# Attention by two pairs of heads at a time, and a float64 conversion with one instruction fewer on ScalarE

## The chip, the cores and the metric

The kernel runs on one core of one Trainium2 chip. The metric is the device time of one execution in microseconds (us). TensorE (PE in the rows) does the matmuls, VectorE (DVE), ScalarE (ACT) and GpSimd (POOL) the elementwise work, and SyncE (SP) issues the DMAs. Each engine works through its own list of instructions in a fixed order; engines wait for one another by semaphores.

## The reference

Three layers in float32, for 4 batches of 448 tokens and a width of 768:

```python
# 1: causal attention, 12 heads of 64
scores = scale * (q @ k.T); scores = where(mask, -1e9, scores); attn = softmax(scores)
x = (attn @ v) -> (batch, 448, 768)
# 2: dense layer with a rotation and a mix over tokens
theta = x @ w_theta
y = w_tok_r @ (x * cos(theta)) + w_tok_i @ (x * sin(theta))
u = x + y
x = u + maximum(u @ w_ch, 0)
# 3: four experts, each an attention of one head; two per token by a gate
logits = x @ w_gate; w = softmax over the two largest
out = sum over experts of w_e * (causal attention(x wq_e, x wk_e, x wv_e) @ wo_e)
```

`w_theta`, `w_ch` and the two token matrices come as float64, everything else as float32.

## The kernel before

**Stages.** For each batch b the kernel runs `attn1(b)` (six pairs of heads), `dense1(b)` (theta, token mixing, channel matmul, then values, gate, queries and keys of the experts) and `attn2(b)` (two pairs of experts, then the output matrices). The first attention of batch b+1 and the second attention of batch b-1 are interleaved with the dense layer of batch b. So the program starts with an attention that has no dense layer beside it, goes through a long stretch of dense matmuls with attention between them, and ends with a second attention. What is called the head below is the stretch until the token mixing of batch 0 runs: attention of batch 0, theta of batch 0, and the conversion of the weights that these need.

**Arithmetic.** The dense matmuls split each float32 operand in a high and a low part of a faster type and do three products (`mm3`). The scores, transposes and `attn @ v` are plain float32 matmuls, which the trace records as two passes each.

**One pair of heads** is `pair`, line 606. The 448 rows of queries are cut in chunks of 128, 128, 128 and 64 (0 to 3). Chunk c needs only the first 128(c+1) keys. Queries and keys of one head fill 64 partitions, so two heads stand on the two halves of a tile `raw`, and their score matmuls (64 rows each) are issued in twos, into two PSUM banks `sc`. `scores([2])` does chunk 2 of both heads (384 columns), then chunk 3 of both heads goes into one full matmul (448 columns), then `scores([1, 0])` does chunks 1 and 0 (256 + 128 columns). After each, DVE takes mask and maximum (`CUSTOM_DVE_ANT_0`), ACT the exponent, and ACT or POOL the scaling by the reciprocal sum. Then follow transposes (`tp`), copies to `ph`, and `attn @ v` into `av`.

**Float64 weights.** `widen`, line 543, turns 384 (or 448) float64 numbers per partition, read as pairs of 32-bit words, into a high and a low float32 part. It runs 24 times for `w_theta` and `w_ch` (tile `c`, 384 wide) and 7 times for the token matrices (tile `zt`, 448 wide). Its steps: ACT scales the upper word; DVE shifts the exponent into place and adds the sign (`cmb`); DVE masks the mantissa in SBUF; ACT turns it into a float between 1 and 2 in the PSUM bank `cv`; DVE adds the lower word; DVE or POOL multiplies by the power (the combine); then come the high part (a copy on any of three engines) and the low part (a subtraction). The bank `cv` is also that of the transposes `zn<-cv` in the dense layer.

**Order.** Nothing is issued as written. `Plan` collects steps, gives each a due time (`rank`, line 298), and `issue` (line 312) plays through a list schedule with a cost for each instruction (`cost`); where a step has several engines to choose from (copies, scalings, combines) it takes the one that would end first. The order on every engine is fixed by that when the program is built. The numbers in `K` (line 489) shift due times. Its cost for a `tensor_scalar` on DVE is the fast one unless an input lies in PSUM; where the output lies is not asked.

Of the kernel before, what the change touches and what calls it, by code (L numbers as in the profile page):

```python
# [480 lines left out]
class Engine:  # L481
# [3 lines left out]
    def __getattr__(self, method):  # L485
        return lambda *a, **kw: self._plan.add(self._name, method, *a, **kw)


K = {"path": 1.62, "hop": -40.0, "slack": 10.0, "war": 300.0, "ahold": 41390.0, "f1": 0.03, "f2": 0.79, "f3": 1.13,
# [4 lines left out]


# [1 line left out]
def dense_sparse_attention_kernel(ctx: ExitStack, tc: tile.TileContext, qk, v, w64, w32, wo, wvg, wtok, out):  # L497
# [7 lines left out]
    pe, act, dve, pool, sp = (Engine(plan, n) for n in ("tensor", "scalar", "vector", "gpsimd", "sync"))  # L505

    BUFS = {"unit": 6, "hl": 12, "zt": 6, "zn": 3, "xt": 2 * NK, "c1": 4, "raw": 3, "vt": 2,
            "qp": 3, "v2": 4, "pa": 3, "pc": 2, "ph": 3, "cmb": 2, "st": 9, "gt": 2, "sm": 2}
    PBUFS = {"sc": 2, "tp": 2, "av": 1, "mm": 2, "cv": 1}

    def sbt(shape, dtype, tag):
# [2 lines left out]
    def pst(tag):  # L514
        return plan.tile(psp, [P, 512], F32, tag, PBUFS[tag], psum=True)
# [27 lines left out]
    def widen(raw, n, hi, lo):  # L543


        e_ = raw[:, :n, 1]
        act.activation(e_.f32(), e_.f32(), AF.Copy, scale=REBIAS)
        e_ = e_.bitcast(U32)
        p_ = sbt([S], F32, "cmb")[:, :n]
        dve.tensor_scalar(p_.bitcast(U32), e_, 3, 0x7F800000, op0=OP.logical_shift_left, op1=OP.bitwise_and)  # L550
        plan.claim(hi)
        dve.scalar_tensor_tensor(p_.bitcast(U32), e_, 0x80000000, p_.bitcast(U32), op0=OP.bitwise_and, op1=OP.bitwise_or)
        dve.tensor_scalar(e_, e_, 0xFFFFF, None, op0=OP.bitwise_and)
        x_ = pst("cv")[:, :n]
        act.activation(x_, e_, AF.Copy, scale=2.0 ** -20, bias=1.0)
        y_ = e_.bitcast(F32)
        dve.scalar_tensor_tensor(y_, raw[:, :n, 0].bitcast(U32), LOWBIT, x_, op0=OP.mult, op1=OP.add)
        plan.combine(p_, y_, p_, OP.mult, "vg")
        plan.copy(hi, p_, "sgv")
        plan.combine(lo, p_, hi.f32(), OP.subtract, "gv")  # L560

# [44 lines left out]
    def pair(raw, vts, gate, dest, due, gap, tag=lambda name: name):  # L606


        plan.due = due
        raw = raw()  # L610
        qs = [raw[64 * j:64 * j + 64, :512] for j in range(2)]
        ks = [raw[64 * j:64 * j + 64, 512:] for j in range(2)]
        sums = sbt([7], F32, "st")
        bias = sbt([7], F32, "st")
        rec = sbt([7], F32, "st")
        ps = [sbt([768], F32, tag("pa")) for _ in range(2)]
        pc = sbt([512], F32, "pc")
        pool.memset(pc[:, S:], 0.0)

        def softmax(sc_, p, n, m, col):  # L620
            dve.tensor_tensor_reduce(out=p, in0=sc_, in1=m, scale=-0.125, scalar=3.0e38,
                                     op0=OP.add, op1=OP.min, accum_out=bias[:, col:col + 1])
            act.activation(p, p, AF.Exp, bias=bias[:, col:col + 1], scale=-1.0, accum_out=sums[:, col:col + 1])

        def part(j, c):
            return ps[j][:, SECS[c]:SECS[c] + 128 * (c + 1)]

        def scores(chunks):
            banks = [pst("sc") for _ in range(2)]
            plan.group()  # L630
            at = 0
            for c in chunks:
                n = 128 * (c + 1)
                for j in range(2):
                    pe.matmul(banks[j][:, at:at + n], qs[j][:, 128 * c:128 * c + 128], ks[j][:, :n], start=True, stop=True)
                at += n
            plan.end_group()
            at = 0
            for c in chunks:
                n = 128 * (c + 1)  # L640
                for j in range(2):
                    softmax(banks[j][:, at:at + n], part(j, c), n, mask[:, 512 - n:512], 2 * (2 - c) + j)
                at += n

        def norm(a, b_, items):
            dve.tensor_scalar(rec[:, a:b_], sums[:, a:b_], 1e-9, None, op0=OP.add)
            dve.reciprocal(rec[:, a:b_], rec[:, a:b_])
            if gate is not None:
                dve.tensor_tensor(rec[:, a:b_], rec[:, a:b_], gate[:, a:b_], op=OP.mult)
            for p, col in items:  # L650
                plan.scale(p, p, rec[:, col:col + 1])

        scores([2])
        norm(0, 2, [(part(j, 2), j) for j in range(2)])
        plan.due = due + K["f1"] * gap
        sc_ = pst("sc")
        pe.matmul(sc_[:, :S], raw[:, 384:512], raw[:, 512:], start=True, stop=True)
        softmax(sc_[:, :S], pc[:, :S], S, mask3, 6)
        scores([1, 0])
        norm(2, 7, [(pc[:, :S], 6)] + [(part(j, c), 2 * (2 - c) + j) for c in (1, 0) for j in range(2)])  # L660
        plan.due = due + K["f2"] * gap

        def blk(who, c, kc):
            if who == 2:
                return pc[:, kc * 128:kc * 128 + 128]
            return ps[who][:, SECS[c] + kc * 128:SECS[c] + kc * 128 + 128]

        banks = [(0, 1, [(0, 2, 0), (1, 2, 0), (2, 3, 0), (2, 3, 3)]), (1, 1, [(2, 3, 1), (0, 2, 2), (1, 2, 2), (2, 3, 2)]),
                 (0, 0, [(0, 0, 0), (1, 0, 0), (0, 1, 0), (1, 1, 0)]), (1, 0, [(0, 1, 1), (1, 1, 1), (0, 2, 1), (1, 2, 1)])]
        parts = [sbt([1024], F32, tag("ph")) for _ in range(2)]  # L670
        for t, i, blocks in banks:
            tp = pst("tp")
            at = 0
            for who, c, kc in blocks:
                if who == 2:
                    pe.transpose(tp[:, at:at + 128], blk(who, c, kc), ident)
                    at += 128
                else:
                    place = tp[:, at:at + 256].rearrange("p (h j d) -> p h j d", h=2, j=2)
                    pe.transpose(place[:, :, who], blk(who, c, kc), ident)  # L680
                    at += 256 * who
            plan.copy(parts[t][:, 512 * i:512 * i + 512], tp)
        plan.due = due + K["f3"] * gap
        SRC = [(0, 0), (1, 0), (1, 640), (0, 896)]
        o_ = pst("av")
        plan.group()
        for kc in range(4):
            n = S - 128 * kc
            for j in range(2):
                t, at = SRC[kc]  # L690
                p = parts[t][:, at:at + 2 * n].rearrange("p (b j d) -> p b j d", j=2, d=64)[:, :, j]
                pe.matmul(o_[64 * j:64 * j + 64, kc * 128:S], vts[j][:, kc], p, start=(kc == 0), stop=(kc == 3))
        plan.end_group()
        plan.completes(o_[:, :S])
        if dest is not None:
            plan.copy(dest, o_[:, :S])
        h_ = sbt([S], F32R, "hl")
        l_ = sbt([S], F32R, "hl")
        plan.copy(h_, o_[:, :S])
        dve.tensor_tensor(l_, o_[:, :S], h_.f32(), op=OP.subtract)  # L700
        return h_, l_

    xhl = {}
    x0 = {}

    def attn1(b, due0, gap):
        for pr in range(H // 2):
            due = due0 + pr * gap

            def fetch():  # L710
                raw = sbt([512 + S], F32, "raw")
                plan.after = max(0.0, due - K["ahold"])
                sp.dma_start(raw, qk[b, pr])
                plan.after = 0.0
                return raw

            plan.due = due
            vt = sbt([2, 4, D], F32, "vt")
            sp.dma_start(vt, v[b, pr])
            xp = sbt([S], F32, "xt")  # L720
            count = [0]

            def tag(name):
                if b == 0 and name == "pa":
                    count[0] += 1
                    return ("pa", "zn")[count[0] % 2]
                return name

            x0[b, pr] = xp
            xhl[b, pr] = pair(fetch, [vt[:, j] for j in range(2)], None, xp, due, gap, tag)  # L730

    def mm3(o, ws, rhs, nk):
        i = 0
# [176 lines left out]
    def attn2(b, due0, gap):  # L910
        qps, v2, g7 = st2[b]
        hl = []
        for r in range(2):
            due = due0 + r * gap
            hl.append(pair(lambda: qps[r], [v2[r][:, :, j] for j in range(2)], g7[:, r, :], None, due, gap))
        banks = K["wom"] if b == B - 1 else K["wo2"] if b == B - 2 else "a"
        names = {"a": "av", "m": "mm", "s": "sc", "t": "tp", "v": "av"}
        for m in range(NK):
# [83 lines left out]
```

## Time and profile before

| | |
|---|---|
| median of 3 runs | 672.63 us (671.33 to 673.14) |
| the profiled execution | 672.36 us |
| its span, first to last instruction | 670.6 us |
| PE busy in the span | 642.0 us (96%) |
| DVE busy | 424.3 us (63%) |
| ACT busy | 391.9 us (58%) |
| POOL busy | 114.4 us (17%) |
| mean granted TensorE clock | 0.992 of full speed |

The shares are means over unlike stages: in the head DVE and ACT are busy all the time and PE is not, in the long middle PE is. Busy times count overlapping parts of neighbouring instructions twice, so for a sum on a full engine the distance from start to start of two rows is used. The profiled execution is within the spread of the three runs.

### The profile page before, as it was taken

The page shows a single profiled execution, that of the slowest core. Times are in us where ns is not written, and L with a number is a line of the kernel's source. Part 1 is how long each engine was busy: PE and PEld are TensorE (multiplying, and loading weights), DVE is VectorE, ACT ScalarE, POOL GpSimd, SP SyncE. Part 2 cuts the span into 40 slices and gives each one's busy share as a digit, 9 for nine tenths or more (in the row PEclk, how much of TensorE's full clock was granted, in tenths as well). Part 3 has the DMA queues.
Part 4 walks back from the last instruction along what each step waited for, and adds up shares of the span by engine and source line. Part 5 has one row for each costly group of instructions (what it writes and reads, how often), then busy time and mean ns, then how long its engine had stood idle before and what let it go on. Part 6 is the DMA issues. An engine that isn't in the chain of part 4 may idle for free.

```text
span 670.6 us, 11048 instructions
## 1 busy us (share of the span) xinstructions
PE 642.0 (96%) x3728; PEld 520.5 (78%) x3728; DVE 424.3 (63%) x1325; ACT 391.9 (58%) x976; POOL 114.4 (17%) x224
## 2 busy tenths in 40 slices
PE   7997779999999999999999999999999999999987
PEld 5564567878797879887787778888878888998865
DVE  4999999999955685544526686553633567434251
ACT  5999788786813684444547677444555374105274
POOL 3542212222400120011001123001101012001010
PEclk9999789999999999999999999999999999999999
DMA  8846640355878624246546543415541750064253
GB/s 329 310 139 201 206 134 29 110 163 187 285 230 291 212 91 147 91 140 177 166 98 211 168 134 85 133 36 163 169 122 49 258 157 11 24 222 119 63 173 117
DMA packets 46184, 103.13 MB, mean 154 GB/s; under 512 B 4784, under 2 KB 16560, under 8 KB 46128
## 3 DMA queue, kind: packets, MB, share of 16 engines
q1 hardware_dynamic: 46128, 102.43, 48.0%
q8 instruction: 29, 0.48, 0.3%
q14 instruction: 27, 0.22, 0.1%
HBM read 81.15 MB, written 21.26 MB: 153 GB/s over the span
## 4 chain that ended last, share of the span: by engine, by line
PE 81%; DVE 8%; ACT 6%; DMA 3%; issue 1%; POOL 0%; ACTq 0%; SPq 0%; POOLq 0%; DVEq 0%
PE mm L478 53%; PE av L478 10%; PE sc L478 8%; PE tp L478 7%; PE cv L478 3%; DVE cmb L478 2%; ACT pa L478 2%; DMA unit<-scr 2%; ACT zn L478 1%; DVE zt L478 1%; DVE zn L478 1%; ACT ph L478 1%; DVE c L478 1%; ACT pc L478 1%; DVE pa L478 1%
## 5 line engine op out<-in xcount | busy, mean ns | idle before, releaser
L478 PE MATMUL mm<-zt,unit 128*128 128x448 f32 x720 | 161.4, 374 | 0.0
L478 ACT ACTIVATE pa<-pa,st 128x384 f32<-128x384 f32 (+2 forms) x265 | 126.6, 493 | 59.4 <-DVE st L478 55.3
L478 PEld LDWEIGHTS mm<-zt,unit 128*128 128x128 f32 x720 | 132.3, 188 | 16.6 <-issue 5.0
L478 PE MATMUL mm<-wt,zn 128*128 128x448 f32 x504 | 126.9, 380 | 0.6 <-ACT zn L478 0.5
L478 PE MATMUL mm<-hl,unit 128*128 128x448 f32 x432 | 102.8, 383 | 7.4 <-DVE zt L478 4.8
L478 PEld LDWEIGHTS mm<-wt,zn 128*128 128x128 f32 x504 | 90.0, 188 | 13.8 <-issue 3.1
L478 PEld LDWEIGHTS mm<-hl,unit 128*128 128x128 f32 x432 | 80.5, 192 | 21.2 <-DVE zt L478 6.6
L478 POOL TENSOR_SCALAR pa<-pa,st 128x384 f32<-128x384 f32 (+2 forms) x83 | 45.1, 551 | 267.6 <-DVE st L478 196.5
L478 DVE CUSTOM_DVE_ANT_0 pa<-sc,mask 128x384 f32<-128x384 f32 (+1 forms) x174 | 66.7, 418 | 36.8 <-PE sc L478 31.9
L478 ACT ACTIVATE ph<-tp 128x512 f32<-128x512 f32 x100 | 55.0, 593 | 29.8 <-PE tp L478 29.5
L478 PE MATMUL sc<-raw 64*128 64x384 f32 (+3 forms) x336 | 68.3, 432 | 1.4 <-DVE st L478 1.2
L478 PE MATMUL tp<-ident,pa 128*128 128x128 f32 x348 | 59.7, 279 | 5.0 <-POOL pa L478 5.0
L478 PEld LDWEIGHTS tp<-ident,pa 128*128 128x128 f32 x348 | 44.1, 143 | 12.9 <-POOL pa L478 6.6
L478 DVE TENSOR_TENSOR zn<-cv,zn 128x512 fp32r<-128x512 f32 (+1 forms) x48 | 29.8, 621 | 32.5 <-ACT zn L478 32.2
L478 PE MATMUL av<-ph,vt 128*64 128x448 f32 (+3 forms) x384 | 46.8, 386 | 2.2 <-ACT xt L478 2.2
L478 ACT ACTIVATE pc<-pc,st 128x448 f32<-128x448 f32 x51 | 34.1, 669 | 24.6 <-DVE st L478 23.9
L478 PEld LDWEIGHTS av<-ph,vt 128*64 128x64 f32 x384 | 25.4, 136 | 27.7 <-issue 13.3
L478 PEld LDWEIGHTS sc<-raw 64*128 64x128 f32 (+1 forms) x336 | 33.5, 187 | 12.4 <-issue 6.9
L478 PE MATMUL mm<-unit,zt 128*128 128x260 f32 (+1 forms) x264 | 36.9, 289 | 0.3 <-DMA unit<-scr 0.3
L478 PEld LDWEIGHTS mm<-unit,zt 128*128 128x128 f32 (+1 forms) x264 | 33.1, 183 | 4.2 <-issue 2.4
L478 ACT ACTIVATE zn<-cv 128x512 fp32r<-128x512 f32 (+1 forms) x34 | 18.5, 543 | 26.1 <-PE cv L478 25.9
L478 DVE SCALAR_TENSOR_TENSOR xt<-mm,xt 128x448 f32<-128x448 f32 x24 | 14.9, 620 | 29.3 <-PE mm L478 29.3
(121 smaller groups left out, 900.2 us busy)
## 6 DMA issues: line engine op xcount, KB each, us to landing
unit<-scr SPq DMA_DIRECT2D x96, 384.0 KB, 3.5
scr<-unit SPq DMA_DIRECT2D x32, 384.0 KB, 3.2
raw<-qk SPq DMA_DIRECT2D x24, 480.0 KB, 4.2
c<-w SPq DMA_DIRECT2D x24, 384.0 KB, 3.5
vt<-v SPq DMA_DIRECT2D x24, 256.0 KB, 2.9
unit<-scr SPq DMA_DIRECT2D x18, 260.0 KB, 3.1
c<-scr SPq DMA_DIRECT2D x18, 256.0 KB, 2.9
out<-cmb SPq DMA_DIRECT2D x18, 224.0 KB, 2.7
```

The lines of the kernel that those rows point to most:

```text
L478: getattr(getattr(self.nc, engine), name)(*args, **kw)
```

## The change

Four things change together.

1. In the first attention two pairs of heads are built by one call (`double`): the second chunks (chunk 1) of both pairs, four matmuls of 256 columns, form one group of score matmuls in one couple of banks. Chunk 0 moves to the group of chunk 2 (384 + 128 columns). The second attention uses the same `pair` through `single`, with groups of chunks 2 and 0, and of chunk 1 alone.
2. `widen` no longer makes a mantissa. The shifted upper word, with its 20 bits of mantissa, is kept as it is; one DVE `tensor_scalar` takes sign and exponent of it into the PSUM bank `cv`; the lower word is multiplied by that, and the combine is an addition. The ACT instruction into `cv` is gone; the DVE instruction that masked the mantissa in SBUF is replaced by the one that writes `cv`.
3. The tile `pa` gets four buffers in place of three.
4. The numbers in `K` are others.

```diff
-K = {"path": 1.62, "hop": -40.0, "slack": 10.0, "war": 300.0, "ahold": 41390.0, "f1": 0.03, "f2": 0.79, "f3": 1.13,
+K = {"path": 1.62, "hop": -200.0, "slack": 10.0, "war": 300.0, "ahold": 42240.0, "f1": -0.16, "f2": 1.27, "f3": 1.14,
...
         p_ = sbt([S], F32, "cmb")[:, :n]
-        dve.tensor_scalar(p_.bitcast(U32), e_, 3, 0x7F800000, op0=OP.logical_shift_left, op1=OP.bitwise_and)
+        dve.tensor_scalar(p_.bitcast(U32), e_, 3, 0x7FFFFFFF, op0=OP.logical_shift_left, op1=OP.bitwise_and)
         plan.claim(hi)
         dve.scalar_tensor_tensor(p_.bitcast(U32), e_, 0x80000000, p_.bitcast(U32), op0=OP.bitwise_and, op1=OP.bitwise_or)
-        dve.tensor_scalar(e_, e_, 0xFFFFF, None, op0=OP.bitwise_and)
         x_ = pst("cv")[:, :n]
-        act.activation(x_, e_, AF.Copy, scale=2.0 ** -20, bias=1.0)
+        dve.tensor_scalar(x_.bitcast(U32), p_.bitcast(U32), 0xFF800000, None, op0=OP.bitwise_and)
         y_ = e_.bitcast(F32)
-        dve.scalar_tensor_tensor(y_, raw[:, :n, 0].bitcast(U32), LOWBIT, x_, op0=OP.mult, op1=OP.add)
-        plan.combine(p_, y_, p_, OP.mult, "vg")
+        dve.scalar_tensor_tensor(y_, raw[:, :n, 0].bitcast(U32), LOWBIT, x_, op0=OP.mult, op1=OP.mult)
+        plan.combine(p_, y_, p_, OP.add, "vg")
...
-        scores([2])
+        second = yield qs, ks
+        if second is not None:
+            soft(second, 256, 1)
+        banks = scores([2, 0], [(qs, ks)] * 2)
+        soft(banks, 0, 2)
         norm(0, 2, [(part(j, 2), j) for j in range(2)])
+        soft(banks, 384, 0)
         plan.due = due + K["f1"] * gap
+        if second is None:
+            mine = yield
+            banks = scores([1] * len(mine), mine)
+            soft(banks, 0, 1)
+            yield banks
         sc_ = pst("sc")
         pe.matmul(sc_[:, :S], raw[:, 384:512], raw[:, 512:], start=True, stop=True)
         softmax(sc_[:, :S], pc[:, :S], S, mask3, 6)
-        scores([1, 0])
...
+    def double(a, b):
+        ga, gb = pair(*a), pair(*b)
+        ma = next(ga)
+        ga.send(None)
+        due = plan.due
+        mb = next(gb)
+        plan.due = due
+        banks = ga.send([ma, mb])
+        first = next(ga)
+        plan.due = b[4]
+        return first, gb.send(banks)
...
+        for pr in range(0, H // 2, 2):
+            xhl[b, pr], xhl[b, pr + 1] = double(*jobs[pr:pr + 2])
```

The number of matmuls, of DMAs and of bytes is the same in both kernels; the order on every engine is another.

On PE, the last score group before the second group of the token mixing of batch 0 stands like this in the kernel before (`mm_1302` and `mm_1352` are the first and second group of the token mixing, `sc` the score banks):

```order
L478 MATMUL mm_1302<-wt_502,zn_1296 128x448
L478 MATMUL mm_1352<-wt_502,zn_1334 128x448
L478 MATMUL sc_1357<-raw_956 128x256
L478 MATMUL sc_1358<-raw_956 128x256
L478 MATMUL sc_1357<-raw_956 128x128
L478 MATMUL sc_1358<-raw_956 128x128
L478 MATMUL mm_1302<-wt_502,zn_1296 128x448
```

In the changed kernel the last one before that place stands just ahead of the first transposes of the dense layer (`cv`), between transposes of the attention (`tp`):

```order
L478 MATMUL tp_1193<-ident_111,pa_919 128x2x64
L478 MATMUL tp_1193<-ident_111,pc_833 128x128 x2
L478 MATMUL sc_1199<-raw_941 128x256
L478 MATMUL sc_1200<-raw_941 128x256
L478 MATMUL sc_1199<-raw_1058 128x256
L478 MATMUL sc_1200<-raw_1058 128x256
L478 MATMUL tp_1210<-ident_111,pc_833 128x128
L478 MATMUL tp_1210<-ident_111,pa_919 128x2x64
L478 MATMUL tp_1210<-ident_111,pc_833 128x128
L478 MATMUL cv_1217<-ident_111,zt_914 128x128 x4
```

One group held 256 and 128 columns of one `raw`; it now holds 256 columns of one `raw` and 256 of the next, and needs both to be loaded.

On DVE, at the end of the head, the kernel before finishes the last token matrix (`zt_768`, its part in `cv_1319` written by ACT) ahead of the third low half of the transposed tiles (`zn_1334`):

```order
L478 SCALAR_TENSOR_TENSOR zt_768<-zt_768,cv_1319 128x448
L478 SCALAR_TENSOR_TENSOR zt_1309<-zt_1309,mm_1219 128x448
L478 TENSOR_TENSOR cmb_1197<-zt_768,cmb_1197 128x448
L478 TENSOR_SCALAR zt_1309<-zt_1309 128x448
L478 CAST wt_502<-cmb_1197 128x448
L478 ISA pa_1350,st_1216<-sc_1147,mask_67 128x384
L478 ISA st_1216 128x1
L478 TENSOR_TENSOR wt_502<-cmb_1197,wt_502 128x448
L478 TENSOR_TENSOR zn_1334<-cv_1333,zn_1334 128x512
```

The changed kernel does the last token matrix (`zt_811`) like this, at about the same place of its list:

```order
L478 TENSOR_SCALAR cv_1270<-cmb_1178 128x448
L478 TENSOR_SCALAR zt_1206<-zt_1206 128x448
L478 SCALAR_TENSOR_TENSOR zt_811<-zt_811,cv_1270 128x448
L478 TENSOR_SCALAR zt_1214<-zt_1214 128x448
L478 TENSOR_TENSOR cmb_1178<-zt_811,cmb_1178 128x448
L478 ISA pa_1143,st_1144<-sc_1199,mask_67 128x256
L478 ISA st_1144 128x1
L478 CAST wt_672<-cmb_1178 128x448
L478 ISA pa_1187,st_1144<-sc_1200,mask_67 128x256
L478 ISA st_1144 128x1
L478 TENSOR_TENSOR wt_672<-cmb_1178,wt_672 128x448
```

DVE now writes `cv` itself, right before it reads it, and no instruction of ACT stands between.

## Rows read from the trace of the kernel before

**Rows 1.** Windows by stage: busy us (and count) of each engine, granted clock, DMA.

```profile
23.00:65.00 42.00, 37.43 (x245) 23.93 (x243) 39.79 (x136) 41.11 (x120) 17.05 (x29) 1.00 0.57 188
65.00:111.50 46.50, 36.99 (x181) 29.43 (x181) 45.80 (x121) 35.66 (x74) 7.23 (x11) 0.89 0.41 136
111.50:150.00 38.50, 38.37 (x227) 30.84 (x226) 37.90 (x105) 31.05 (x75) 12.04 (x16) 1.00 0.39 124
150.00:640.00 490.00, 486.94 (x2837) 405.90 (x2836) 278.09 (x864) 250.50 (x620) 65.49 (x130) 1.00 0.47 146
640.00:671.00 31.00, 23.75 (x140) 18.01 (x138) 8.10 (x38) 17.61 (x42) 3.01 (x6) 1.00 0.48 157
```

**Rows 2.** Timeline of PE around 111 us: start, us, instruction [idle before <-releaser].

```profile
109.82 0.89 PE L478 MATMUL mm<-wt,zn 128*128 128x448 f32 x3 [0.48 <-ACT zn L478]
111.49 0.47 PE L478 MATMUL mm<-wt,zn 128*128 128x448 f32 x1
112.05 3.32 PE L478 MATMUL mm<-wt,zn 128*128 128x448 f32 x15
```

**Rows 3.** Timeline of DVE, 84 to 111 us, in pieces.

```profile
84.20 0.36 DVE L478 TENSOR_SCALAR c<-c 128x384 uint32<-128x384 uint32 x1
84.46 0.55 DVE L478 TENSOR_TENSOR unit<-cmb,unit 128x384 fp32r<-128x384 f32 x1
84.93 0.42 DVE L478 CUSTOM_DVE_ANT_0 pa<-sc,mask 128x256 f32<-128x256 f32 x1
...
85.28 0.55 DVE L478 SCALAR_TENSOR_TENSOR c<-c,cv 128x384 f32<-128x384 uint32 x1
85.74 0.39 DVE L478 TENSOR_SCALAR cmb<-zt 128x448 uint32<-128x448 uint32 x1
...
91.41 0.62 DVE L478 TENSOR_SCALAR zt<-mm 128x448 f32<-128x448 f32 x1
91.95 0.62 DVE L478 TENSOR_TENSOR cmb<-zt,cmb 128x448 f32<-128x448 f32 x1
92.48 0.62 DVE L478 SCALAR_TENSOR_TENSOR zt<-zt,mm 128x448 f32<-128x448 f32 x1
...
93.55 0.39 DVE L478 TENSOR_SCALAR zt<-zt 128x448 uint32<-128x448 uint32 x1
93.85 0.39 DVE L478 TENSOR_SCALAR cmb<-zt 128x448 uint32<-128x448 uint32 x1
...
110.77 0.68 DVE L478 TENSOR_TENSOR zn<-cv,zn 128x512 fp32r<-128x512 f32 x1
```

**Rows 4.** Timeline of PE, 152 to 171 us: groups of score matmuls between dense ones.

```profile
152.19 0.92 PE L478 MATMUL sc<-raw 64*128 64x256 f32 x8
153.04 1.49 PE L478 MATMUL mm<-zt,unit 128*128 128x448 f32 x6
154.47 1.95 PE L478 MATMUL av<-ph,vt 128*64 128x448 f32 x16
156.35 6.37 PE L478 MATMUL mm<-zt,unit 128*128 128x448 f32 x30
...
168.22 0.91 PE L478 MATMUL sc<-raw 128*128 128x448 f32 x2
169.06 1.95 PE L478 MATMUL av<-ph,vt 128*64 128x448 f32 x16
```

**Rows 5.** Groups of instructions by form, ACT: busy us, mean ns.

```profile
L478 ACT ACTIVATE cv<-c 128x384 f32<-128x384 uint32 x24 | 12.6, 524 | 5.2 <-DVE c L478 4.4 <-DVE zn L478 0.8
L478 ACT ACTIVATE cv<-zt 128x448 f32<-128x448 uint32 x7 | 4.0, 573 | 1.8 <-DVE zt L478 1.1 <-DVE zn L478 0.6
```

**Rows 6.** The page's DMA issues: KB each, us from issue to landing.

```profile
raw<-qk SPq DMA_DIRECT2D x24, 480.0 KB, 4.2
```

**Rows 7.** Groups by form, POOL: the combine of a conversion.

```profile
L478 POOL TENSOR_TENSOR cmb<-c,cmb 128x384 f32<-128x384 f32 x4 | 4.1, 1030 | 0.0
```

**Rows 8.** Timeline of DVE at 557 us.

```profile
557.37 1.28 DVE L478 TENSOR_TENSOR zt<-xt,zt 128x448 fp32r<-128x448 f32 x1
```

More of the change, by code (lines that the diff above doesn't have):

```diff
@@ L507, in dense_sparse_attention_kernel @@
     BUFS = {"unit": 6, "hl": 12, "zt": 6, "zn": 3, "xt": 2 * NK, "c1": 4, "raw": 3, "vt": 2,
-            "qp": 3, "v2": 4, "pa": 3, "pc": 2, "ph": 3, "cmb": 2, "st": 9, "gt": 2, "sm": 2}
+            "qp": 3, "v2": 4, "pa": 4, "pc": 2, "ph": 3, "cmb": 2, "st": 9, "gt": 2, "sm": 2}
     PBUFS = {"sc": 2, "tp": 2, "av": 1, "mm": 2, "cv": 1}
@@ L626, in part, with scores @@
             return ps[j][:, SECS[c]:SECS[c] + 128 * (c + 1)]
-        def scores(chunks):
+        def scores(chunks, mine):
             banks = [pst("sc") for _ in range(2)]
@@ L631, in scores, with soft @@
             at = 0
-            for c in chunks:
+            for c, (q_, k_) in zip(chunks, mine):
                 n = 128 * (c + 1)
                 for j in range(2):
-                    pe.matmul(banks[j][:, at:at + n], qs[j][:, 128 * c:128 * c + 128], ks[j][:, :n], start=True, stop=True)
+                    pe.matmul(banks[j][:, at:at + n], q_[j][:, 128 * c:128 * c + 128], k_[j][:, :n], start=True, stop=True)
                 at += n
             plan.end_group()
[L638 to L643, printed above, removed]
+            return banks
+        def soft(banks, at, c):
+            n = 128 * (c + 1)
+            for j in range(2):
+                softmax(banks[j][:, at:at + n], part(j, c), n, mask[:, 512 - n:512], 2 * (2 - c) + j)
         def norm(a, b_, items):
@@ L700, in pair, with single @@
         dve.tensor_tensor(l_, o_[:, :S], h_.f32(), op=OP.subtract)
-        return h_, l_
+        yield h_, l_
+    def single(*args):
+        g = pair(*args)
+        mine = next(g)
+        g.send(None)
+        g.send([mine])
+        return next(g)
+    def double(a, b):
[9 more added lines that the diff above has]
+        return first, gb.send(banks)
     xhl = {}
@@ L706, in attn1, with fetch @@
     def attn1(b, due0, gap):
+        jobs = []
         for pr in range(H // 2):
             due = due0 + pr * gap
-            def fetch():
+            def fetch(pr=pr, due=due):
                 raw = sbt([512 + S], F32, "raw")
@@ L721, in attn1, with tag @@
             count = [0]
-            def tag(name):
+            def tag(name, count=count):
                 if b == 0 and name == "pa":
@@ L729, in attn1 @@
             x0[b, pr] = xp
-            xhl[b, pr] = pair(fetch, [vt[:, j] for j in range(2)], None, xp, due, gap, tag)
+            jobs.append((fetch, [vt[:, j] for j in range(2)], None, xp, due, gap, tag))
+        for pr in range(0, H // 2, 2):
+            xhl[b, pr], xhl[b, pr + 1] = double(*jobs[pr:pr + 2])
     def mm3(o, ws, rhs, nk):
@@ L914, in attn2 @@
             due = due0 + r * gap
-            hl.append(pair(lambda: qps[r], [v2[r][:, :, j] for j in range(2)], g7[:, r, :], None, due, gap))
+            hl.append(single(lambda: qps[r], [v2[r][:, :, j] for j in range(2)], g7[:, r, :], None, due, gap))
         banks = K["wom"] if b == B - 1 else K["wo2"] if b == B - 2 else "a"
```

6 rows, old and new, of the table K are left out of this document.

## The prediction

> **What bounds the kernel now.** I read the windows by stage first. From 150 to 640 us PE is busy 486.9 of 490 us at full clock, so only 3.1 us there can be won by filling gaps; in the last 31 us PE is idle for 7.25 [rows 1]. The head is different: from 65 to 111.5 us DVE is busy 45.8 of 46.5, PE 37.0 at a mean clock of 0.89, and from 23 to 65 us ACT is busy 41.1 and DVE 39.8 of 42 [rows 1]. So DVE with ACT sets the head, PE all that follows.
>
> Where one hands over to the other stands in the timelines. PE begins the second group of the token mixing at 109.82, having waited 0.48 us for ACT's high half `zn`; the lo part needs the third low half, which DVE writes from 110.77 to 111.45, and PE goes on with it at 112.05 and runs 3.3 us without a break [rows 2, 3]. After that PE is busy 38.37 of 38.5 us up to 150 [rows 1]. That low half I call the handover. The model is therefore: new time = old time + what DVE has more to do before its third `zn` low half + what PE has more to do behind it. Work of PE ahead of the handover is free, because PE has 9.5 us idle between 65 and 111.5 [rows 1].
>
> **PE.** The 3250 matmuls are the same ones. In the order, runs of 64-row score matmuls fall from 63 to 51, twelve fewer: in each of 4 batches three couples of pairs need three runs where they needed four. What a run costs beyond its columns: one of 384 columns for each head takes 0.85 us from start to start (152.19 to 153.04), and an `av` run of 1024 columns 1.88 (154.47 to 156.35) [rows 4]. That is 1.03 us for 640 columns, 1.61 ns each, and 0.85 − 384 × 0.00161 = 0.23 us for the run itself. Twelve runs are 2.8 us; the bounds are nothing (the 0.23 is all in the first column's latency and stays with the merged runs) and 2.8. I take 2.8, since both rows are neighbours of the same dense matmuls.
>
> Not all of it lies behind the handover. Ahead of that place the changed order has one 448-column score matmul of 128 rows less (0.84 us, 168.22 to 169.06 [rows 4]), one couple of 256-column ones more (256 × 1.61 ns = 0.41), and three score runs fewer (0.69): PE does 1.1 us less there, which is free anyway. Of the saving, −2.8 + 1.1 = −1.7 remains behind it. A group of both pairs also waits for the second pair's `raw`, and behind it in PE's list stand the 128-row scores and transposes of the first pair. A load takes 4.2 us [rows 6] and is issued long ahead of its due time (`ahold` in `K` is 42,240 ns), in a list of SP that has as many entries as before: I cost that wait at nothing. If the load came only with the group, it would cost up to 4.2 us once, in the first couple.
>
> **DVE up to the handover.** By then both orders have all 12 conversions of `w_theta` and all 7 of the token matrices. In each, the mantissa `tensor_scalar` in SBUF, 0.26 us for 384 columns (84.20 to 84.46) and 0.30 for 448 (93.55 to 93.85), gives way to one that writes PSUM [rows 3]. No row of before shows a `tensor_scalar` with its output in PSUM. Below, it stays at 0.26 and 0.30. Above, it goes like the instructions with an input in PSUM: 0.46 (85.28 to 85.74) and 0.54 (91.41 to 91.95) [rows 3]. I take the upper end: the nearest row is `zt<-mm`, the same operation with one of its two tiles in PSUM. Then 12 × 0.20 + 7 × 0.24 = +4.1; at the lower end 0.
>
> [...]
>
> The rest, counted in the two orders up to the third low half, with start-to-start durations of [rows 3]:
> - combines: 8 to 6 of 384 columns and 7 to 3 of 448 go from DVE to POOL: 2 × 0.47 (84.46 to 84.93) + 4 × 0.53 (91.95 to 92.48) = −3.1;
> - one low half of a token matrix less, −0.5, and one product with `xt` less, −0.5;
> - copies: `unit` two more (2 × 0.26), `zn` one more (0.6), `wt`, `hl`, `xt`, `ph` one less each (0.3 and 3 × 0.54): −0.8;
> - masks with maximum: two of 128 and three of 256 columns more, one of 448 less. 256 columns take 0.35 us (84.93 to 85.28), so by columns 576 × 1.37 ns = +0.8;
> - steps of the next conversions that already stand ahead of it: two shifts and one sign, +1.0, and small ones +0.1.
>
> Sum with the slow write: 4.1 − 3.1 − 1.0 − 0.8 + 0.8 + 1.1 = +1.1; with the fast one −3.0.
>
> **ACT.** It loses 24 × 0.524 + 7 × 0.573 = 16.6 us [rows 5], of which 12 × 0.524 + 7 × 0.573 = 10.3 in the head. I cost this at nothing: in the 46.5 us ahead of the handover DVE has 0.7 us left [rows 1], so an ACT that is earlier finds DVE as late as before. POOL's six more combines are costed at nothing too, in the 64 of 88.5 us that it is idle from 23 to 111.5 [rows 1]; rival B is what happens if that cover fails. Four buffers of `pa` and `cv` held shorter only take waits away, of which neither DVE nor PE has any to speak of.
>
> **The sum.** +1.1 − 1.7 = −0.6 us. The profiled execution took 672.36, of which 670.6 are the span and 1.8 lie around it; it is 0.3 under the median of 672.63. So 672.36 − 0.6 = 671.8. About 0.3%, 2.0 us, is what a measurement of this kernel can tell from no change.
>
> **Rivals.**
> - A, the write to PSUM is fast. −3.0 − 1.7 = −4.7: 667.7. For it speaks only that no row shows a slow one; against it `zt<-mm`.
> - B, POOL's combines slow DVE. A combine takes POOL 1.03 us [rows 7]. A DVE operation with two sources that met a POOL instruction took 1.28 us instead of 0.62 [rows 8], 0.66 more. Six more combines ahead of the handover are 6 × 0.66 = +4.0, on the engine that has no slack: 672.36 − 0.6 + 4.0 = 675.8. It decides from +2.6 on (2.0 past the −0.6), when four of the six meet such an operation (2.64). For it: DVE works without a pause there. Against: half of DVE's instructions in [rows 3] are of other kinds, and POOL did similar combines already. [...]
> - C, ACT did hold the head. From 23 to 65 us it is busy 41.1 of 42, and DVE 2.2 less than the window [rows 1]. If an emptier ACT gives all of that, −0.6 − 2.2 = −2.8: 669.6. Against it: DVE's pauses there are short and spread.
> - D, the merged group saves nothing on PE, so that the change doesn't do what it says: −0.6 + 1.7 = +1.1, 673.5, within the same 0.3%.
>
> The handover could also move to another instruction: the sixth group of theta waits for a bank that the fourth leaves. Counted to there, DVE has 5.7 us more and PE 3.0 more ahead, so that −2.8 − 3.0 = −5.8 is left behind it: −0.1 in all, the same answer by another place.
>
> **How the numbers follow.** My forecast with D has 0.44, A 0.18, C 0.17, B 0.21. A is faster by over 0.3%; C lies at the edge, so 0.12 of it goes to faster and 0.05 to the same; of the forecast with its own range of 670.1 to 673.6, 0.06 falls on faster and 0.38 on the same; B gives slower, with 0.01 of it left to the same. That makes 0.36, 0.44 and 0.20. The time is 671.8. For the range I go to just below A and to B: 667.2 to 676.0; the tail of the kernel, whose 7.25 idle us [rows 1] may come out 1.5 us to either side with another order, is within that.
>
> **What would show it.** The `tensor_scalar` that writes `cv`: 0.55 and 0.62 us of duration if the write is slow, 0.36 and 0.39 if fast. The third `zn` low half of DVE: at about 112.5 us by the forecast, about 108.4 by A, 109 to 110 by C, 116 by B, then with many DVE instructions of two sources at 1.0 to 1.3 us beside POOL's combines. PE busy about 639 to 640 instead of 642.0, and after the handover still without gaps. ACT's instructions into `cv` gone and its busy time some 376 to 380. The forecast is wrong if PE idles longer than 3 us in the middle, if a group of both pairs waits for a DMA, or if the end after 640 us grows.

## The result, and the profile after

The changed kernel took 676.11 us (675.73 to 677.71, 5 runs) against 671.73 (671.33 to 673.14) for the kernel before on the same chip: a ratio of 1.0067, 95% interval 1.0048 to 1.0085, so 4.5 us slower. A second group of runs gave 1.0055 (1.0035 to 1.0076). The forecast was 671.8 with a range up to 676.0. The profiled execution of the changed kernel has a span of 673.9 us, 3.3 more than the one of before.

The windows by stage of the changed kernel, columns as in [rows 1]:

```profile
23.00:65.00 42.00, 37.02 (x240) 24.10 (x242) 41.62 (x135) 37.34 (x109) 19.31 (x31) 1.00 0.65 211
65.00:111.50 46.50, 34.71 (x167) 26.38 (x164) 45.97 (x115) 30.18 (x72) 15.70 (x18) 0.85 0.37 121
111.50:150.00 38.50, 38.50 (x224) 32.34 (x223) 37.10 (x94) 25.30 (x58) 11.96 (x16) 1.00 0.33 106
150.00:640.00 490.00, 486.19 (x2837) 406.40 (x2835) 282.77 (x863) 248.71 (x618) 61.83 (x127) 1.00 0.48 147
```

From 65 to 111.5 us POOL is busy 15.70 us where it was 7.23 in [rows 1], ACT has become emptier, DVE is full, and PE does 2.3 us less at a lower mean clock. Behind that PE is full, as before.

The forecast's own yardstick, the third low half `zn` of DVE, ended at 111.45 us [rows 3]. It now ends at 117.08:

```profile
116.39 0.69 DVE L478 TENSOR_TENSOR zn<-cv,zn 128x512 fp32r<-128x512 f32 x1
```

To that instruction I took DVE's time apart: every instruction at the usual start-to-start time of its form, what it takes beyond that ("stretch"), and pauses, in us from DVE's first instruction on.

| | ends | usual work | stretches | pauses |
|---|---|---|---|---|
| before | 110.6 | 97.0 | 1.9 | 11.7 |
| changed | 116.2 | 98.0 | 6.2 | 12.1 |

The work grew by 1.0 us; the forecast had 1.1. The stretches grew by 4.3; the forecast had costed them at nothing. From the third low half to the last instruction it was 670.6 − 111.45 = 559.15 us before and 673.9 − 117.08 = 556.8 now: 2.3 us less, where the forecast had 1.7. Together +5.6 − 2.3 = +3.3, the difference of the spans, as it would be at any instant; whether PE still waits at this one is looked at below.

Where the stretches are, two timelines of the changed kernel show side by side. DVE's, two rows around 70 us and two where PE waits for DVE:

```profile
68.77 0.83 DVE L478 TENSOR_SCALAR st<-st 128x2 f32<-128x2 f32 x1
...
72.44 0.85 DVE L478 TENSOR_SCALAR cmb<-c 128x384 uint32<-128x384 uint32 x1
...
99.70 0.96 DVE L478 SCALAR_TENSOR_TENSOR cmb<-zt,cmb 128x448 uint32<-128x448 uint32 x1
100.58 3.56 DVE L478 TENSOR_TENSOR zt<-zt,xt 128x448 f32<-128x448 f32 x3
```

POOL's at the same times:

```profile
68.42 1.15 POOL L478 TENSOR_TENSOR cmb<-zt,cmb 128x448 f32<-128x448 f32 x1
...
71.92 1.15 POOL L478 TENSOR_TENSOR wt<-cmb,wt 128x448 fp32r<-128x448 f32 x1
...
99.02 1.16 POOL L478 TENSOR_TENSOR cmb<-zt,cmb 128x448 f32<-128x448 f32 x1 [1.97 <-issue]
100.14 1.52 POOL L478 TENSOR_TENSOR zt<-zt,xt 128x448 f32<-128x448 f32 x1
101.59 0.15 POOL L478 MEMSET pc<- 128x64 f32 x1
101.69 1.43 POOL L478 TENSOR_TENSOR zt<-zt,xt 128x448 f32<-128x448 f32 x1
```

Each long DVE instruction begins while a POOL instruction runs. A shift of 384 columns takes 0.85 us where an instruction of that form takes 0.36 [rows 3], a `tensor_scalar` of two columns 0.83 in place of 0.16, three products with `xt` 3.56 in place of 1.7. In the first 113 us there are 12 such meetings with 6.3 us in the changed kernel, 5 with 1.75 in the one before; every one has a POOL instruction beside it. In all 17 the stretch is what is left of POOL's instruction when DVE's begins, less 0.13 to 0.15 us: the POOL instruction of 71.92 runs 0.63 us more at 72.44, and the shift takes 0.49 more. One kind is spared: in the changed kernel's first 113 us 45 DVE instructions with a tile in PSUM begin when a POOL instruction has more than 0.15 us to run, and none of them takes over 0.03 us more than usual. What in the hardware holds the others back, the trace does not show.

PE around the last pause of the head, its timeline in the changed kernel:

```profile
93.47 3.97 PE L478 MATMUL mm<-hl,unit 128*128 128x448 f32 x18 [1.14 <-DVE zt L478]
...
105.87 0.70 PE L478 MATMUL cv<-ident,zt 128*128 128x128 f32 x3 [1.66 <-DVE zn L478]
106.38 1.91 PE L478 MATMUL tp<-ident,pa 128*128 128x128 f32 x8
107.94 4.64 PE L478 MATMUL mm<-hl,unit 128*128 128x448 f32 x18
112.42 0.78 PE L478 MATMUL mm<-wt,zn 128*128 128x448 f32 x3
```

Two windows of the same kernel there, columns as above:

```profile
105.00:110.00 5.00, 4.13 (x18) 3.92 (x19) 5.00 (x12) 4.93 (x12) 0.00 (x0) 0.66 0.00 0
110.00:115.00 5.00, 5.00 (x27) 4.56 (x26) 4.30 (x15) 3.43 (x12) 0.74 (x1) 1.00 0.00 0
```

PE's last wait is no longer at the third low half but at 105.87, for the bank that the first one leaves; PE has the sixth theta group still ahead of it there. That first low half in DVE's timeline, before and changed:

```profile
103.69 0.67 DVE L478 TENSOR_TENSOR zn<-cv,zn 128x512 fp32r<-128x512 f32 x1
105.14 0.68 DVE L478 TENSOR_TENSOR zn<-cv,zn 128x512 fp32r<-128x512 f32 x1
```

It ends 1.5 us later (105.82 against 104.36), and all 12 meetings lie ahead of it. From there to the end it is 568.1 us in place of 566.2, 1.8 more. And PE starts the sixth group at a granted clock of 0.66 in the mean of these 5 us, with 0.50 from 107 to 109 us and 1.00 from 110: the 18 matmuls take 4.48 us from start to start, the fifth group's 18 took 3.80 at full clock (1.00 from 93 to 98 us).

### The profile page after: what moved, and what is told of

Same layout as the page of the kernel before. It is cut to its first block, busy times and chain, and to the rows that moved or that the text cites. A ratio compares the mean times of both kernels' runs of the same rounds, so it can differ in the third digit from the quotient of the medians.

```text
span 673.9 us, 10984 instructions
## 1 busy us (share of the span) xinstructions
PE 642.8 (95%) x3728; PEld 523.3 (78%) x3728; DVE 431.6 (64%) x1317; ACT 375.2 (56%) x947; POOL 121.5 (18%) x230
## 4 chain that ended last, share of the span: by engine, by line
PE 78%; DVE 17%; ACT 3%; issue 2%; DMA 1%; POOL 0%; SPq 0%; DVEq 0%; POOLq 0%
PE mm L478 52%; PE av L478 9%; PE sc L478 8%; PE tp L478 6%; DVE cmb L478 4%; PE cv L478 3%; DVE cv L478 2%; DVE zt L478 2%; DVE pa L478 2%; DVE c L478 1%; ACT pa L478 1%; DVE zn L478 1%; DVE unit L478 1%; DVE st L478 1%; DVE hl L478 1%
## 5 line engine op out<-in xcount | busy, mean ns | idle before, releaser
L478 PE MATMUL mm<-zt,unit 128*128 128x448 f32 x720 | 158.8, 372 | 0.0
L478 ACT ACTIVATE pa<-pa,st 128x256 f32<-128x256 f32 (+2 forms) x261 | 124.2, 491 | 53.9 <-DVE st L478 49.8
L478 PE MATMUL mm<-wt,zn 128*128 128x448 f32 x504 | 120.9, 378 | 0.0
L478 PE MATMUL mm<-hl,unit 128*128 128x448 f32 x432 | 100.3, 383 | 5.5 <-ACT hl L478 1.8
L478 DVE CUSTOM_DVE_ANT_0 pa<-sc,mask 128x384 f32<-128x384 f32 (+2 forms) x174 | 67.0, 418 | 24.3 <-PE sc L478 21.6
L478 POOL TENSOR_SCALAR pa<-pa,st 128x256 f32<-128x256 f32 (+2 forms) x87 | 46.7, 548 | 181.0 <-DVE st L478 132.5
L478 ACT ACTIVATE ph<-tp 128x512 f32<-128x512 f32 x103 | 57.7, 592 | 26.8 <-PE tp L478 26.4
L478 PEld LDWEIGHTS sc<-raw 64*128 64x128 f32 (+1 forms) x336 | 35.1, 192 | 26.2 <-DVE st L478 11.3
L478 ACT ACTIVATE pc<-pc,st 128x448 f32<-128x448 f32 x55 | 36.7, 668 | 21.2 <-DVE st L478 21.0
L478 ACT ACTIVATE zn<-cv 128x384 fp32r<-128x384 f32 (+1 forms) x36 | 19.3, 535 | 34.6 <-PE cv L478 34.3
```

The source lines that it names most:

```text
L478: getattr(getattr(self.nc, engine), name)(*args, **kw)
```

## Experiments

Theory 1 was: POOL's instructions stretch DVE's in the head, and the late head is the whole loss. Its rivals: DVE's own work with the slow write into PSUM; the start of the attention; PE's low clock. Since any edit makes the planner order everything anew, seven kernels keep an order that is already planned, and only what is emitted from it differs. For those, the shift of DVE's instructions against the kernel whose order it is (at 121 us, and at the end of the profile) shows where the time goes, which a median does not; from 121 us to about 500 the shift of the kernels with edits in the head stays constant within 0.4 us.

| replay | ratio to before (95%) | stretches to 113 us | shift at 121 | at the end |
|---|---|---|---|---|
| changed, again | 1.0055 (1.0035–1.0076) | 6.3 | +1.2 | +1.4 |
| short POOL, 12 | 1.0002 (0.9987–1.0017) | 2.7 | −3.2 | −1.7 |
| short combines, 10 | 1.0045 (1.0030–1.0060) | 4.4 | −0.8 | +1.0 |
| two products on DVE | 1.0055 (1.0039–1.0072) | 4.5 | −0.5 | +1.7 |
| `cv` in SBUF | 1.0051 (1.0033–1.0070) | 7.7 | 0.0 | +2.3 |
| short POOL and SBUF | 0.9982 (0.9966–0.9998) | 3.9 | −3.5 | −2.9 |
| groups apart | 1.0103 (1.0083–1.0122) | 5.6 | −1.0 | +3.5 |
| before + six on POOL | 1.0036 (1.0022–1.0050) | 5.7 | +3.1 | +2.9 |

The row "changed, again" is the noise: 0.4 us at the first loads and 0.8 at a lower clock between 80 and 100 us (0.85 and 0.50 from 80 to 85 and 85 to 90, where the first profile has 1.00 and 0.66). So a shift of up to about 1.2 us in one execution shows nothing by itself. Four replays lose 1.5 us near 550 us: the granted clock from 550 to 560 is 0.83 in three of them, and in the changed kernel it is 1.00. In the fourth (short POOL) it is 0.96, and most of the loss lies ahead of 550: from 547.45 us on, 16 of the 18 matmuls that take 3.96 us in the changed kernel take 4.99.

**The twelve in-place POOL instructions shortened.** In `_emit`, before a call is issued (shortened; the columns from 64 on are left out of the result):

```python
+if engine == "gpsimd" and name == "tensor_tensor" and in_place and self.short > 0:
+    self.short -= 1
+    args = [a[:, :64] for a in args]
```


> The changed kernel with every list of instructions as it is, but the first twelve two-source POOL instructions that work in place (ten combines of conversions and two products with x) do 64 columns in place of 384 or 448; the rest of their result is left out. Theory 1 (DVE is stretched where a POOL instruction runs beside it; the trace shows 12 such meetings with 6.3 us in the changed kernel's first 113 us against 1.75 in the one before): the stretches fall by 4.1 us and the time from 676.1 to 672.0 (670.5 to 673.5). Theory 2 (the head is longer through its own work: the slow PSUM writes and the start of the attention): at most 0.7 us less, 675.4 or more.

Measured: 1.0002 (673.73 us against 673.27 for the kernel before in the same group; the expected 672.0 was counted from 671.73), so the loss of 0.55 to 0.67% is gone, and DVE is 3.2 us earlier from 121 us on. The stretches fell by 3.6 us where 4.1 was expected. The same products on DVE as above, in its timeline:

```profile
100.23 1.68 DVE L483 TENSOR_TENSOR zt<-zt,xt 128x448 f32<-128x448 f32 x3
```

And PE behind them:

```profile
103.77 0.55 PE L483 MATMUL cv<-ident,zt 128*128 128x128 f32 x3 [1.40 <-DVE zn L483]
104.28 1.14 PE L483 MATMUL tp<-ident,pa 128*128 128x128 f32 x8
105.36 3.97 PE L483 MATMUL mm<-hl,unit 128*128 128x448 f32 x18
```

1.68 us for three in place of 3.56, and this time PE has the full clock (1.00 from 100 to 110 us, 18 matmuls in 3.80 us). The sixth group is done 3.3 us earlier (109.16 in place of 112.42): 2.1 of them are PE's wait, which ends at 103.77 in place of 105.87, and 1.2 are the clock, for from there to the end of the group PE takes 5.39 us in place of 6.55. So theory 1 holds for the larger part; the low clock went with the stretches here, and the run does not show that it went because of them. The short instructions also hand on POOL's results earlier; the next run has no such side.

**Six more POOL instructions in the kernel before.** After each of the first six low halves of token matrices (shortened): `+nc.gpsimd.tensor_tensor(spare, hi, lo, op=OP.add)`.

> The kernel before with all lists as they are and six more two-source POOL instructions of 448 columns, each released by a low half of a token matrix; their results are used by nobody. Theory 1: each lies beside a DVE that never pauses and stretches it by 0.3 to 0.7 us: +2.0 to +4.0, 673.7 to 675.7. If POOL's instructions cost DVE nothing that counts: within 0.7 us of the kernel before, 671.0 to 672.4.

Measured: 1.0036, 2.4 us, DVE 3.1 us late at 121 us and 2.9 at the end. DVE's timeline beside two of the six:

```profile
94.42 1.33 DVE L479 TENSOR_SCALAR cmb<-zt 128x448 uint32<-128x448 uint32 x1
...
96.75 1.33 DVE L479 TENSOR_SCALAR cmb<-zt 128x448 uint32<-128x448 uint32 x1
```

And POOL's:

```profile
94.35 1.15 POOL L483 TENSOR_TENSOR spare<-wt 128x448 f32<-128x448 f32 x1 [2.36 <-DVE wt L479]
96.43 1.40 POOL L483 TENSOR_TENSOR spare<-wt 128x448 f32<-128x448 f32 x1 [0.93 <-DVE wt L479]
```

A shift that usually takes 0.39 takes 1.33: 0.94 more beside POOL instructions of 1.15 and 1.40 us. No part of the change is in this kernel and nobody reads the six results, so the price belongs to the meeting alone.

**Which of the twelve?** The combines alone shortened, and the two products with `x` moved to DVE at their place:

> As the first kernel with short POOL instructions, but only the ten combines are cut to 64 columns; the two products with x keep their 448. The rest of the combines' result is left out. Rival B as it was written (the combines are what stretches DVE): 4 us less than the changed kernel, as with all twelve cut. By the meetings in the trace, combines have 2.2 us and the two products 1.9: 2.2 us less, some 674.

> The changed kernel with the first two products with x moved from POOL to DVE at the same place in the order. By the meetings in the trace DVE loses 1.9 us of stretches and gains 2 x 0.53 of work: 0.8 us less at the handover, 675 us. If POOL's help is worth its column count (no price for meetings): 1.1 us more, 677.

Measured: stretches 1.9 us fewer in the first, 1.8 in the second, as the meetings said; but DVE gained only 0.8 and 0.5 at 121 us, which is within the noise, and the medians moved within their intervals. In both the granted clock from 105 to 110 us was 0.66 again. PE's sixth theta group, combines short and then products on DVE:

```profile
106.44 5.37 PE L483 MATMUL mm<-hl,unit 128*128 128x448 f32 x18 [0.17 <-DVE zt L483]
106.75 5.28 PE L482 MATMUL mm<-hl,unit 128*128 128x448 f32 x18 [1.17 <-DVE zt L482]
```

PE's wait for the bank ends earlier in both (104.85 and 104.09 in place of 105.87), but the group takes 5.37 and 5.28 us in place of 4.64. So what each kind of the twelve is worth in time is not shown; only the stretches part them.

**The write into `cv`.** Shortened: `+if t.tag == "cv" and step.engine == "vector": where, tag = sb, "x0"`.

> The changed kernel with every list as it is, but the DVE instruction that takes sign and exponent writes to SBUF, and the instruction behind it reads it there. Theory 1 alone (stretches by POOL, DVE's own work as forecast): the 18 conversions ahead of the point where PE stops waiting give back 12 x 0.20 + 6 x 0.24 = 3.8 us of DVE: 672.3, with the instruction at 0.36 and 0.39 us. Theory 3 (the late end of the head comes from PE's low clock and from waits for PE, not from DVE): 675 or more.

The groups by form (count, busy us, mean ns), in the changed kernel and in this one:

```profile
L478 DVE TENSOR_SCALAR cv<-cmb 128x384 uint32<-128x384 uint32 x24 | 13.3, 554 | 0.1
L478 DVE TENSOR_SCALAR cv<-cmb 128x448 uint32<-128x448 uint32 x7 | 4.3, 614 | 0.0
L481 DVE TENSOR_SCALAR cv<-cmb 128x384 uint32<-128x384 uint32 x24 | 9.4, 391 | 0.1
L481 DVE TENSOR_SCALAR cv<-cmb 128x448 uint32<-128x448 uint32 x7 | 2.6, 377 | 0.0
```

And its windows of 100 to 110 us:

```profile
100.00:105.00 5.00, 2.39 (x10) 1.34 (x10) 5.00 (x7) 3.40 (x9) 2.06 (x3) 0.52 0.01 3
105.00:110.00 5.00, 5.00 (x19) 4.70 (x19) 5.00 (x14) 4.88 (x13) 0.00 (x0) 0.50 0.00 0
```

The instruction is about as fast as said (391 and 377 ns), but the expected 3.8 us did not come; with 1.0051 and 676.83 us the run came out by its other branch, 675 or more through PE. Stretches grew to 7.7 us: two readers of `cv`, which now take both tiles from SBUF, were held beside POOL (0.32 and 0.35 us; the means of their forms rose from 548 to 581 ns and from 611 to 664), and other instructions met it at their new times. And PE ran at half clock from 100 to 110 us (0.52 and 0.50). With the twelve short as well:

> Twelve POOL instructions cut to 64 columns (the rest of their result is left out) and the sign and exponent written to SBUF, all lists as in the changed kernel. The slow write is 0.20 or 0.24 us in 18 conversions ahead of the handover: 3.6 us less than with the short instructions alone, some 669, if DVE alone sets the head. If PE's low clock or its own waits take it back, as seen with the SBUF write alone: under 1.5 us less, 671 or more.

Measured: 0.9982, and at 121 us 0.3 us more than the short ones alone. DVE's first low half begins 1.5 us earlier than with the short ones alone (101.50 against 103.04), but from the first transposes behind it to the end of the sixth group PE takes 5.97 us in place of 4.88, at a granted clock of 0.73 from 100 to 105 us. So the slow write is real, some 4 us of work as forecast, and in this execution the clock took back most of what the head won without it. The stretches here are 3.9 us and the clock is low all the same.

**The merged groups taken apart.** One PE step is emitted between the two halves of each group (shortened, the condition in words):

```python
+if len(calls) == 4 and all(c is a 256-column score matmul for c in calls):
+    calls, self.held = calls[:2], calls[2:]
```


> The changed kernel with one matmul or transpose of PE put between the two halves of each merged group of second chunks; all other lists as they are. 62 runs of 64-row score matmuls in place of 51, nine of them in batches 1 to 3 where PE has no pauses. The forecast's price of 0.23 us for a run: 2.1 us more between 130 us and the end, 678 us. If a merged run saves nothing: within 0.5 us of the changed kernel there.

PE's timeline at 403 us in the changed kernel:

```profile
403.26 1.14 PE L478 MATMUL sc<-raw 64*128 64x256 f32 x8
404.33 0.68 PE L478 MATMUL mm<-hl,unit 128*128 128x448 f32 x2
```

And with the group apart:

```profile
403.43 0.70 PE L489 MATMUL sc<-raw 64*128 64x256 f32 x4
404.06 0.47 PE L489 MATMUL mm<-hl,unit 128*128 128x448 f32 x1
404.45 0.70 PE L489 MATMUL sc<-raw 64*128 64x256 f32 x4
405.09 0.47 PE L489 MATMUL mm<-hl,unit 128*128 128x448 f32 x1
```

Halves take 0.63 and 0.64 against 1.07 together, 0.20 more, and the one dense matmul between them 0.39 where it takes about 0.2 in a row (18 in 3.80 us, as above). The shift of PE steps up by 0.39 to 0.40 at four such places (162, 300, 340 and 403 us), by 0.31 where a transpose stands between. At the first of the four the 0.40 is gone again by 170 us, behind a group for which PE waited 0.20 us in the changed kernel. Two places cost 1.48 each, because an `av` run of 1.88 us was put in and the next softmax came too late (a wait of 1.21 for DVE). So a run costs 0.40 between dense matmuls and 0.31 by a transpose, not 0.23; how much of that a kernel keeps depends on the waits behind it.

**Orders made anew.** One part undone or done alone, with numbers in `K` that belong to other code:

> The changed kernel with one line of the planner: a tensor_scalar or copy on DVE whose output lies in PSUM is charged at the slow rate. The order changes. Theory 1 with the reason that the plan runs ahead of the chip and so puts POOL's instructions into gaps that are not there: stretches fall from 6.3 us to under 3.5, and with 2.6 us less of DVE's work ahead of the third low half (95.7 against 98.3 counted in the order) the time is 671 (669 to 673.5). If the wrong charge does not matter: 675 to 677.

> The changed kernel with the old float64 conversion (mantissa in SBUF, ACT writes cv); pairs by two, four buffers and the new numbers stay. The order changes: two-source instructions on POOL fall from 43 to 32, DVE's counted work to its first low half from 87.9 to 87.0. Theory 1: stretches of DVE at most half of the 6.3 us, 672.0 (670.5 to 673.5). If the pairs by two or the new numbers make the head late: 675 or more.

> The kernel before (old conversion, numbers and three buffers) with pairs by two in batches 1 to 3 only, where PE has no pauses: 54 runs of 64-row score matmuls in place of 63. At 0.23 us each 9 runs are 2.1 us on a busy PE; DVE's counted work to the third low half 96.5 against 97.2. So 2 to 3 us less than the kernel before, 669.5 (668 to 671). If a merged run saves nothing: within 1 us of before.

> The kernel before with the new conversion alone. 63 runs of score matmuls, so nothing is saved on PE; DVE's counted work to the fourth theta is 90.9 us against 83.8, to the third low half 102.7 against 97.2. Theory 1 with the forecast's count of DVE's work: 3 to 7 us slower than before, 675 to 679, with stretches of over 3 us. If the conversion is not what makes the changed kernel slow: within 1.5 us of before.

> The changed kernel itself once more, beside the others of this group: 0.5 to 0.8% over the kernel before, with stretches of DVE of 6 us in the first 113 us.

Measured: 1.0082 (1.0065–1.0098), 1.0133 (1.0108–1.0158), 1.0139 (1.0114–1.0164) and 1.0163 (1.0136–1.0190); the changed kernel again 1.0055. The first four missed the time they were to have, and not by the parts they undid: stretches fell to 2.9, 1.8, 2.7 and 3.6 us, but in the first three DVE's pauses grew to 16.1, 19.3 and 15.7 us in the first 113 (11.9 in the changed kernel); where the fourth lost its time was not taken apart. The old conversion came out by its other branch, 675 or more, but with a new order that does not put the loss on the couples or the numbers. With the old conversion DVE paused 18.9 us to its first low half (11.3 in the changed kernel), and PE had one wait of 4.87 us, in its timeline:

```profile
80.79 0.90 PE L478 MATMUL tp<-ident,pc 128*128 128x128 f32 x3 [4.87 <-POOL pc L478]
```

Such a run says what an unfitted order costs, here 5 to 11 us, and nothing of the part.

**Numbers fitted to each code.** With the slow write charged and 0.20 us for each change between 64-row and other matmuls, `K` was chosen anew for three codes by the planner's own length:

> All edits of the change, with the planner charged the slow rate for DVE instructions that write PSUM and 0.20 us for each change of PE between 64-row and other matmuls (0.40 a run, as the taken-apart groups showed), and with numbers in K that make the planned length 656.0 us; with the change's own numbers the same charges plan 668.2. The kernel with the true DVE charge alone took 678.5. If the chip stays behind the plan by the same distance: 666 (663 to 670), 2 to 8 us under the kernel before. If stretches of DVE by POOL come whatever is planned: 672 or more, with 6 us of them in the head.

> As the last, with another set of numbers in K found for the same charges: planned length 657.1 us. By the same distance 667 (664 to 671). The two sets together show how far one can go by the plan alone: they should lie within 3 us of each other; if the order's luck with stretches and PE's clock decides, they lie further apart.

> Pairs by two with the old float64 conversion, same charges, numbers in K chosen for this code: planned 657.9 us. By the same distance 668 (665 to 672). If the new conversion is worth something on the chip, slower than the first of these by about 2 us; if it only moves work to DVE, not slower.

> The code of the kernel before (pairs one by one, old conversion) with the same charges and numbers in K chosen for it: planned 661.2 us. By the same distance 671 (668 to 674), so no better than the kernel before; the difference to the pairs by two is then what 12 runs fewer give, 3 to 5 us.

Measured: 1.0086 (1.0059–1.0113), 1.0000 (0.9984–1.0016), 0.9985 (0.9972–0.9999) and 1.0053 (1.0034–1.0071). In us that is 678.61, 672.85, 672.48 and 676.48, where 666, 667, 668 and 671 were expected: the chip did not stay behind the plan by the same distance. The first two carry the same edits, planned 1.1 us apart, and lie 0.86% apart, 5.8 us: the order alone moved more here than the whole change did (4.5 us). And the faster of the two has the more stretches to 113 us, 5.6 us against 4.7, so stretches are one price among several. The couples with the old conversion are the one complete kernel here that comes out under the kernel before, by 0.15%, barely. Against the same code without couples it is 4.0 us faster by the medians, where 12 × 0.40 would be 4.8; but with one set of numbers for each, and 5.8 us between two sets, that is a hint and not shown.

## Why the prediction was wrong, point by point

- **What bounds the kernel, and the sum's form.** DVE up to a handover and PE behind it was right, the place was not. At the third low half the parts are +5.6 and −2.3, but PE no longer waits there; at the first one, behind which it waits no more, they are +1.5 and +1.8. The other handover that the prediction named, the bank that the fourth theta group leaves, was not it either. So that the terms fit at the old place is in part luck.
- **DVE's work.** Right: +1.1 said, +1.0 measured, with the slow write (554 and 614 ns said as 0.55 and 0.62). Rival A is out. The destination, for which the kernel before has no row, now has its own: 554 ns into PSUM and 391 into SBUF for 384 columns, 614 and 377 for 448.
- **PE's saving.** That a merged run saves was right, the size too small: 0.23 us was read from the runs' own rows and left out the neighbour that also slows; taken apart, a run costs 0.40 between dense matmuls. PE's busy time, said to fall from 642.0 to 639 or 640 us, is 642.8 all the same; how much of that is the low clock was not taken apart.
- **The step that failed** is "POOL's six more combines are costed at nothing too, in the 64 of 88.5 us that it is idle". Free time on POOL was no cover, since the price is paid on DVE: +4.3 us. Rival B had the size, 6 × 0.66 = 4.0, and 0.21 of the chance.
- **Rival B's reasons against it** failed too. That half of DVE's instructions are of other kinds was no shelter for those that keep to SBUF: the one-source shifts and the tiny `tensor_scalar` on `st` were stretched as much (0.85 and 0.83 us). The trace of the kernel before had such a meeting already, DVE's timeline and POOL's:

```profile
53.23 0.79 DVE L478 TENSOR_SCALAR st<-st 128x5 f32<-128x5 f32 x1
52.84 1.15 POOL L478 TENSOR_TENSOR wt<-cmb,wt 128x448 fp32r<-128x448 f32 x1 [2.80 <-DVE wt L478]
```

And combines brought 2.2 us of stretches, products with `x` 1.9, so the count of combines that gave 4.0 was right by chance in part. The prediction had booked a product with `xt` that left DVE as 0.5 us won.

- **Left out**: PE's clock. The sixth theta group ran at a mean of 0.66 (105 to 110 us) where PE had become the bound, which cost 1.2 us against the run with short POOL instructions. Whether the stretches bring the low clock is not shown: with the same twelve short and `cv` in SBUF it was low too. Rivals C and D are out: DVE's pauses went from 11.7 to 12.1 us, and the merged groups do save.
- **Open**: why such meetings are few in one order (1.75 us) and many in another (6.3). The plan keeps POOL's instructions apart from those of DVE that its function `locks` names, but that function counts only inputs of over 8 columns, so the `tensor_scalar` on `st` goes free; it makes 4 of the 12 meetings with 2.2 us, and 4 of the 5 before. The other eight are of kinds that the plan excludes, and why they meet on the chip is open. The plan with the true charge had 2.9 us, but was slower elsewhere. The four buffers of `pa` were not tried by themselves.

## What to carry to other kernels

When DVE has no pause, an instruction moved to an idle POOL is not free (here six cost DVE 3.1 us): count the DVE instructions it will run beside that keep to SBUF, one-source ones and tiny ones too, and charge each meeting what is left of POOL's instruction; here 12 meetings in 113 us took 6.3 us, each of them that rest less 0.13 to 0.15 us. To test one part of a kernel whose order is planned, replay the order and change only what is emitted; here a plan made anew moved more time than the part. And where an engine hands over to PE, look at the clock that PE has in the first microseconds behind its last wait (here 0.66, and 1.00 in the run with short POOL instructions).

## What was not expected of the hardware

- A `tensor_scalar` on two columns, 0.16 us alone, took 0.83 beside a POOL combine of 1.15 us; POOL's own products took 1.52 and 1.43 us in the meeting, where one in the kernel before took 1.14.
- A run of 64-row matmuls slows the dense matmul next to it too: 0.39 us for one of 448 columns between two such runs, where one in a row takes about 0.2 (18 in 3.80 us).
- The same order shows a drop of the granted clock near 550 us in some executions and none in others, 1.5 us each time: from 550 to 560 us it was 0.83 in three of the replays and 1.00 in the changed kernel, and in a fourth (short POOL) 16 of the 18 matmuls that took 3.96 us in the changed kernel took 4.99.
